# Four edits to the planner and the loads of a fused attention and MoE kernel: longer planned transfers, filling products on another bank, loads noted two pairs ahead, one-column operations that exclude nothing

## The chip, the cores and the metric

The kernel runs on one core of one Trainium2 chip. The metric is device time in microseconds (us), taken as the median of 3 runs of the kernel. A separate profiled execution gives the trace; its times below count from the first instruction of its span. Engines are named as the profile names them: PE (TensorE matmul), PEld (TensorE weight load), DVE (VectorE), ACT (ScalarE), POOL (GpSimd) and SP (SyncE, which issues every DMA here, one after the other).

## The reference

```
# q, k, v: (4 batches, 8 heads, 576 rows, 64); M_prev: (4, 8, 64, 64); z_prev: (4, 8, 64)
scores = q @ k.T / 8, causal mask, softmax (sum + 1e-9)      -> a
local = a @ v
phi(x) = max(x, 0) + min(exp(x), 1)
mem = (phi(q) @ M_prev) / (phi(q) @ z_prev + 1e-6)
x = gate * mem + (1 - gate) * local          # gate = sigmoid(beta) of each head
x as (2304 tokens, 512)
h = max(x @ w1, x @ w2, x @ w3)              # each w 512 x 768
out = h @ w_out                              # 768 x 512
```

All of it is in float32.

## The kernel before

**Work.** The 576 rows of a batch are cut into a first half of 320 rows and a second of 256. A "pair" is two heads of one half of one batch: 32 pairs, numbered 0 to 31 in the order batch, half, pair of heads, so that pairs 0 to 3 are the first half of batch 0, and pairs 8 to 11 the first half of batch 1. For each pair the kernel loads keys and queries (`load_qk`), transposes them, makes the scores of each head (tile `bs` in PSUM, the masked result and its least value by DVE, the exponential by ACT with its sum, a reciprocal by DVE, the scaling by POOL: tiles `p`, `st`, `sum`), transposes them (PE into `bt`, ACT copies to `pt`) and multiplies them with the values and the memory (`values`, PE into `bv`). What comes out is split into a high part `xh` and a low part `xl`. Pairs 0 to 3 use plain float32 products; from pair 4 on (SPLIT) operands are split into high and low parts; from pair 8 on (FLIP) keys and queries come through the ring `rw` of three buffers (12 transfers for a pair, 32 partitions each) and are turned by DVE (STREAM_TRANSPOSE into `rk`).

**The MoE of a half** can begin when all four of its pairs have their `xh` and `xl`. An "up" item is 12 products of one 128-column block into one PSUM bank, `bm`: three for each of the four pairs of heads (`xh,wh`, `xl,wh`, `xh,wl`). The items are spread between the steps of the next four pairs. Until all weights are there, all items use bank `bm[0]` alone.

**Weights** come in 24 chunks of 512 KB through the same ring `rw`. ACT scales a chunk into a `bm` bank, DVE rebuilds it there in three operations (the last writes `g`), ACT rounds it to `wh` and POOL takes the rest into `wl`. The first 8 chunks (SPREAD, L363) take the three `bm` banks in turn, the later ones only `bm[1]` and `bm[2]` (L550). Six chunks are noted in the steps of pairs 1 to 4, one more with each item of the MoE.

**Order.** Nothing is issued as the code runs: `Plan` notes each operation with what it depends on and a price (`cost`, `move`), and `emit` then plays all five engines forward in planned time and writes out each engine's instructions in that order. An operation is placed as soon as the plan has its inputs ready; the order of noting only decides between those that are ready. Each engine then runs its list in order, so a wrong price in the plan makes an engine wait at an instruction for which others stand ready behind it. L319 gives a transfer its planned landing, L201 its planned time in the DMA engines, `shares` (L204) says which DVE and POOL operations the plan doesn't let run together. Where the plan has PE idle for over 400 ns, L301 puts in small products of no use ("filling products", L300 in the profile) until the first real operation on the tensor that they write has come. Every other instruction of the plan has line L320 in the profile.

Of the kernel before, what the change touches and what calls it, by code (L numbers as in the profile page):

```python
# [17 lines left out]
PSUM = bass.MemoryType.PSUM  # L18


def f(ap):
    return ap.bitcast(F32)
# [45 lines left out]
class Plan:  # L68
# [119 lines left out]
    @staticmethod  # L188
    def move(*aps):

        piece, size = 512, 4
        for d in aps[0].shape:
            size *= d
        for ap in aps:
            run = 4
            for st, n in reversed(ap.ap if ap.space == bass.MemoryType.DRAM else ap.ap[1:]):
                if 4 * st != run:
                    break
                run *= n
            piece = min(piece, run)  # L200
        return size / 360 * (2 if piece < 512 else 1)  # L201

    @staticmethod
    def shares(eng, name, kw):  # L204

        if eng == "pool":
            return True
        if eng != "dve":
            return False
        aps = [a for a in kw.values() if isinstance(a, bass.AP) and a.shape[-1] > 1]  # L210
        inputs = [a for k, a in kw.items() if k in ("in_", "in0", "in1") and a.space != PSUM]
        if len(inputs) > 1:
            return True
        return name in ("tensor_scalar", "tensor_copy") and not any(a.space == PSUM for a in aps)

    def note(self, can):

# [40 lines left out]
    def emit(self):  # L258

        free = dict.fromkeys(self.ENGINES, 0.0)  # L260
        load = dict.fromkeys(self.ENGINES, 0.0)
        heaps = {e: [] for e in self.ENGINES}
        wait = {e: [] for e in self.ENGINES}
        dma = 0.0
        last = 0.0
        port = {"pool": 0.0, "dve": 0.0}
        other = {"pool": "dve", "dve": "pool"}

        def place(op):
            best = None  # L270
            for e, name, kw, cost in op.can:
                ready = max([0.0] + [
                    o.end + self.AFTER[o.eng][e] + self.SLACK * (e == "pe" and o.eng != "pe")
                    for o in op.deps
                ])
                done = max(ready, free[e] + load[e]) + cost + self.PEN.get(e, 0)
                if best is None or done < best[0]:
                    best = done, ready, (e, name, kw, cost)
            _, ready, (op.eng, op.fn, op.args, op.cost) = best
            load[op.eng] += op.cost  # L280
            heappush(wait[op.eng], (ready, op.prio, op.num, op))

        for op in self.ops:
            if not op.left:
                place(op)
        for _ in self.ops:
            start = {}
            for e in self.ENGINES:
                while wait[e] and wait[e][0][0] <= free[e]:
                    op = heappop(wait[e])[3]  # L290
                    heappush(heaps[e], (op.prio, op.num, op))
                if heaps[e]:
                    start[e] = free[e]
                elif wait[e]:
                    start[e] = wait[e][0][0]
            e = min(start, key=start.get)
            if e == "pe" and self.filler:
                free[e] = max(free[e], FILL_FROM)
                while start[e] - free[e] > FILL_GAP:
                    self.nc.tensor.matmul(**self.filler)  # L300
                    free[e] += 215 if free[e] < 4000 else 112  # L301
            if not heaps[e]:
                op = heappop(wait[e])[3]
            else:
                op = heappop(heaps[e])[2]
            op.at = start[e]
            if self.shares(e, op.fn, op.args):
                op.at = max(op.at, port[other[e]])
                port[e] = op.at + op.cost
            if e == "pe":  # L310

                w = op.args["in_" if op.fn == "transpose" else "lhsT"]
                last = op.at = max(op.at, last + 0.835 * w.shape[-1])
            load[e] -= op.cost
            if self.filler and op.args["out"].tensor.name == self.filler["out"].tensor.name:
                self.filler = None
            free[e] = op.end = op.at + op.cost
            if e == "sp":
                dma = op.end = max(op.end + 650, dma) + op.move  # L319
            getattr(getattr(self.nc, self.ENGINES[e]), op.fn)(**op.args)  # L320
            for u in op.users:
                u.left -= 1
                if not u.left:
                    place(u)
        return max(free.values())
# [20 lines left out]
def attention_memory_moe(ctx, tc, q, k, v, m_prev, z_prev, beta, w1, w2, w3, w_out, out):  # L346
# [11 lines left out]
    FLIP, XLOW, PHI, SPLIT = 8, 4, 4, 4  # L358


    EARLY_STEPS, PER_PIECE = range(3, 9), 1

    SPREAD = 8  # L363

    cp = ctx.enter_context(tc.tile_pool(name="cp", bufs=1))
    ps = ctx.enter_context(tc.tile_pool(name="ps", bufs=1, space=PSUM))
# [1 line left out]
    def tile_(shape, dtype, name):  # L368
        return cp.tile(shape, dtype, name=name)

    ident = tile_([128, 128], F32, "ident")
    mask = tile_([128, 448], F32, "mask")
# [39 lines left out]
    b_v = Ring(ps, 1, [128, 512], F32, "bv")  # L412
    bm = Ring(ps, 3, [128, 512], F32, "bm").tiles
# [11 lines left out]
    pairs = [(b, hi, hp) for b in range(B) for hi in range(2) for hp in range(NP)]  # L425
# [48 lines left out]
    def load_z(b):  # L474
        per_batch["z", b] = t = r_z.next()
        P.sp.dma_start(out=t, in_=z_prev[b : b + 1].broadcast_to([128, H, D]))

    def load_mv(b):

        per_batch["mv", b] = t = r_mv.next()  # L480
        P.sp.dma_start(out=t[:D], in_=m_prev[b].rearrange("h d e -> d h e"))
        P.sp.dma_start(out=t[D:], in_=v[b, :, 0:D, :].rearrange("h p d -> p h d"))

    def load_v(pi):
# [14 lines left out]
        out=mask[:, 320:],  # L499
# [43 lines left out]
    def load_weights(n):  # L543

        for _ in range(min(n, len(wchunks))):
            i = 4 * NF - len(wchunks)
            src, dh, dl = wchunks.popleft()
            t = r_w.next()
            g = r_g.next()
            bank = bm[i % 3 if i < SPREAD else 1 + i % 2]  # L550
            tv = t.rearrange("p (t x) -> p t x", t=NP) if len(src.shape) == 3 else t
            gv = g.rearrange("p (t x) -> p t x", t=NP) if len(src.shape) == 3 else g
            P.sp.dma_start(out=tv, in_=src)
            words = t.rearrange("p (x w) -> p x w", w=2)
            bits = bank.bitcast(U32)
            P.act.activation(out=bank, in_=f(words[:, :, 1]), func=AF.Copy, scale=2.0**-111)
            P.dve.tensor_scalar(
                out=bits, in0=bits, scalar1=3, scalar2=None, op0=ALU.logical_shift_left
            )
            P.dve.scalar_tensor_tensor(  # L560
                out=bits, in0=words[:, :, 0], scalar=29, in1=bits,
                op0=ALU.logical_shift_right, op1=ALU.bitwise_or,
            )
            P.dve.scalar_tensor_tensor(
                out=g.bitcast(U32), in0=words[:, :, 1], scalar=0x80000000, in1=bits,
                op0=ALU.bitwise_and, op1=ALU.bitwise_or,
            )
            P.act.copy(out=dh, in_=gv)
            P.pool.tensor_tensor(out=dl, in0=gv, in1=f(dh), op=ALU.subtract)
        if not wchunks and len(b_m.tiles) == 1:  # L570
            b_m.tiles += bm[1:]
            b_m.at = 1
# [348 lines left out]
    def run_moe(budget):  # L921
        while moe_q and budget > 0:
            c, fn = moe_q.popleft()
            load_weights(PER_PIECE)
            fn()
            budget -= c
        return budget
# [7 lines left out]
    transpose_in(0, "k")  # L935
    transpose_in(0, "q")
    debt = 0.0
    for n in range(nheads + 2):
        pieces = []
        sc = pt = None  # L940
        if n < nheads:
            pi, e = heads[n]
            us = HALVES[pairs[pi][1]].units
            sc = [(2 * u[3] * 0.425 + 100, partial(scores, pi, e, u)) for u in us]
            if HALVES[pairs[pi][1]].top and e == 0:
                sc.insert(0, (300, partial(scores_top, pi)))
            if e == 0:
                if pi + 1 < len(pairs):
                    load_qk(pi + 1)
                    b = pairs[pi + 1][0]  # L950
                    if b != pairs[pi][0]:
                        load_z(b)
                        load_mv(b)
        if n in EARLY_STEPS:
            load_weights(1)
# [9 lines left out]
        if n < nheads:  # L965
            pi, e = heads[n]
# [31 lines left out]
    run_moe(1e9)  # L998

    P.filler = dict(  # L1000
        out=b_v.tiles[0][:32, :64], lhsT=mask[:, :32], rhs=mask[:, :64], start=True, stop=True
    )
    P.emit()

# [29 lines left out]
```

## Time and profile before

| | before |
|---|---|
| median of 3 runs | 532.56 us (532.47 to 532.63) |
| the profiled execution | 532.99 us, its span 531.2 us |
| PE busy | 509.4 us, 96% of the span |
| DVE, ACT, POOL busy | 283.8, 336.1, 332.5 us |
| mean granted TensorE clock | 0.978 of 2.4 GHz |

The span is what the trace sees of the execution; 1.8 us lie around it. Busy PE is not PE at its peak: at the low clock the same product is busy for longer. The idle time of an engine costs nothing where another one is the bound.

### The profile page before, as it was taken

The page shows a single profiled execution, that of the slowest core. Times are in us where ns is not written, and L with a number is a line of the kernel's source. Part 1 is how long each engine was busy: PE and PEld are TensorE (multiplying, and loading weights), DVE is VectorE, ACT ScalarE, POOL GpSimd, SP SyncE. Part 2 cuts the span into 40 slices and gives each one's busy share as a digit, 9 for nine tenths or more (in the row PEclk, how much of TensorE's full clock was granted, in tenths as well). Part 3 has the DMA queues.
Part 4 walks back from the last instruction along what each step waited for, and adds up shares of the span by engine and source line. Part 5 has one row for each costly group of instructions (what it writes and reads, how often), then busy time and mean ns, then how long its engine had stood idle before and what let it go on. Part 6 is the DMA issues. An engine that isn't in the chain of part 4 may idle for free.

```text
span 531.2 us, 11153 instructions
## 1 busy us (share of the span) xinstructions
PE 509.4 (96%) x3602; PEld 445.1 (84%) x3602; DVE 283.8 (53%) x1048; ACT 336.1 (63%) x942; POOL 332.5 (63%) x505
## 2 busy tenths in 40 slices
PE   9879999989989899999999999999999999999997
PEld 7545687867978789998899889998899899997996
DVE  3667999987675354465455354445754454240110
ACT  4877989778676485577666586676776565533111
POOL 4777777888686475676787476677866554331110
PEclk9966999999999899999999999999999999999999
DMA  4846666664443564322442244231321110001001
GB/s 119 218 109 154 168 170 188 144 219 89 93 81 69 103 130 89 69 45 57 105 81 52 46 102 90 56 56 40 79 43 23 39 39 23 21 1 39 21 1 40
DMA packets 160090, 44.00 MB, mean 83 GB/s; under 512 B 147104, under 2 KB 156576, under 8 KB 160032
## 3 DMA queue, kind: packets, MB, share of 16 engines
q1 hardware_dynamic: 160032, 43.29, 35.7%
q8 instruction: 28, 0.46, 0.4%
q14 instruction: 30, 0.25, 0.2%
HBM read 38.54 MB, written 4.72 MB: 81 GB/s over the span
## 4 chain that ended last, share of the span: by engine, by line
PE 75%; ACT 6%; DMA 6%; DVE 4%; SPq 4%; issue 2%; POOL 2%; DVEq 0%; POOLq 0%; ACTq 0%
PE bm L320 49%; PE bv L320 9%; PE bt L320 8%; PE bs L320 8%; SPq L320 4%; DMA rw<-in_moe_w_dram 2%; DMA rw<-in_k_dram 1%; DMA rw<-in_q_dram 1%; ACT p L320 1%; PE bv L300 1%; ACT pt L320 1%; DVE g L320 1%; DVE bm L320 1%; ACT wh L320 1%; ACT k L320 1%
## 5 line engine op out<-in xcount | busy, mean ns | idle before, releaser
L320 PE MATMUL bm<-xh,wh 128*128 128x320 f32 (+1 forms) x576 | 178.3, 310 | 3.1 <-DVE t L320 2.2
L320 PE MATMUL bm<-xh,wl 128*128 128x320 f32 (+1 forms) x576 | 171.1, 297 | 0.0
L320 PE MATMUL bm<-xl,wh 128*128 128x320 f32 (+1 forms) x576 | 170.4, 296 | 0.0
L320 PEld LDWEIGHTS bm<-xh,wh 128*128 128x128 f32 x576 | 109.1, 189 | 9.4 <-DVE t L320 3.4
L320 POOL TENSOR_SCALAR p<-p,sum,gb 128x192 f32<-128x192 f32 (+3 forms) x128 | 87.5, 685 | 46.7 <-DVE sum L320 34.5
L320 PEld LDWEIGHTS bm<-xl,wh 128*128 128x128 f32 x576 | 109.2, 190 | 0.2
L320 PEld LDWEIGHTS bm<-xh,wl 128*128 128x128 f32 x576 | 109.0, 189 | 0.1
L320 ACT ACTIVATE p<-p,st 128x192 f32<-128x192 f32 (+4 forms) x144 | 84.7, 588 | 17.6 <-DVE st L320 16.6
L320 DVE TENSOR_TENSOR t<-bm,t 128x320 f32<-128x320 f32 (+1 forms) x96 | 43.4, 452 | 97.4 <-PE bm L320 97.0
L320 PE MATMUL bt<-ident,p 128*128 128x128 f32 x464 | 73.6, 279 | 11.5 <-ACT pt L320 7.9
L320 ACT COPY pt<-bt 128x384 f32<-128x384 f32 (+3 forms) x189 | 74.5, 417 | 10.9 <-PE bt L320 10.2
L320 DVE CUSTOM_DVE_ANT_0 p<-bs,mask 128x192 f32<-128x192 f32 (+3 forms) x128 | 60.1, 472 | 29.6 <-PE bs L320 28.8
L320 PEld LDWEIGHTS bt<-ident,p 128*128 128x128 f32 x464 | 56.4, 142 | 19.2 <-POOL p L320 6.9
L320 PE MATMUL bs<-k,qs 128*128 128x448 f32 (+2 forms) x336 | 69.9, 310 | 1.3 <-DVE st L320 1.1
L320 POOL TENSOR_TENSOR qs<-rk,qs 128x256 fp32r<-128x256 f32 (+1 forms) x42 | 34.2, 816 | 33.6 <-ACT qs L320 18.7
L320 PEld LDWEIGHTS bs<-k,qs 128*128 128x128 f32 x336 | 50.4, 186 | 4.7 <-DVE st L320 2.4
L320 POOL TENSOR_TENSOR hl<-t,hh 128x256 fp32r<-128x256 f32 x42 | 31.0, 739 | 34.1 <-ACT hh L320 34.1
L320 DVE STREAM_TRANSPOSE rk<-rw 128x320 f32<-128x320 f32 (+1 forms) x72 | 34.2, 476 | 30.0 <-POOL qs L320 10.6
L320 POOL TENSOR_TENSOR p<-phf,nn 128x128 f32<-128x128 f32 (+1 forms) x96 | 35.3, 373 | 18.0 <-PE bt L320 15.3
L320 ACT CAST qs<-rk 128x256 fp32r<-128x256 f32 (+1 forms) x47 | 20.1, 431 | 36.1 <-PE bs L320 35.3
L320 PE MATMUL bv<-pt,rv 128*64 128x256 f32 (+1 forms) x384 | 42.4, 352 | 0.0
L320 PEld LDWEIGHTS bv<-pt,rv 128*64 128x64 f32 x384 | 27.9, 141 | 16.9 <-issue 2.9
(91 smaller groups left out, 851.6 us busy)
## 6 DMA issues: line engine op xcount, KB each, us to landing
rw<-in_moe_w_dram SPq DMA_DIRECT2D x18, 512.0 KB, 4.6
rq<-in_q_dram SPq DMA_DIRECT2D x88, 64.0 KB, 2.5
rv<-in_v_dram SPq DMA_DIRECT2D x32, 128.0 KB, 2.9
rw<-in_q_dram SPq DMA_DIRECT2D x96, 40.0 KB, 2.1
out_dram<-g SPq DMA_DIRECT2D x15, 256.0 KB, 2.1
rw<-in_moe_w_out_dram SPq DMA_DIRECT2D x6, 512.0 KB, 4.2
rw<-in_q_dram SPq DMA_DIRECT2D x96, 32.0 KB, 2.0
rv<-in_v_dram SPq DMA_DIRECT2D x32, 64.0 KB, 2.3
```

Of the source, the lines that this page charges most:

```text
L300: self.nc.tensor.matmul(**self.filler)
L320: getattr(getattr(self.nc, self.ENGINES[e]), op.fn)(**op.args)
```

## The change

It makes five edits. `move` prices a transfer with long pieces at 240 bytes per ns where it had 360 (the price of short pieces, 180, stays). L319 lets a transfer land 1200 ns after its issue at the earliest, where it had 650. `shares` now says that an operation all of whose operands are one column wide excludes nothing. All weight chunks take banks `bm[1]` and `bm[2]`, so the first user of `bm[0]` is the MoE, and the filling products write `bm[0]`: they end at its first product instead of the first `values`. From pair 8 on, keys and queries are noted two pairs ahead.

```
-        return size / 360 * (2 if piece < 512 else 1)
+        return size / (180 if piece < 512 else 240)
@@ shares
-        return name in ("tensor_scalar", "tensor_copy") and not any(a.space == PSUM for a in aps)
+        return (
+            name in ("tensor_scalar", "tensor_copy")
+            and bool(aps) and not any(a.space == PSUM for a in aps)
+        )
@@ emit
-                dma = op.end = max(op.end + 650, dma) + op.move
+                dma = op.end = max(op.end + 1200, dma) + op.move
@@
-    SPREAD = 8
@@ load_weights
-            bank = bm[i % 3 if i < SPREAD else 1 + i % 2]
+            bank = bm[1 + i % 2]
@@
+    loaded = 1
@@
             if e == 0:
+                while loaded < min(len(pairs), pi + (3 if pi >= FLIP else 2)):
+                    load_qk(loaded)
+                    loaded += 1
                 if pi + 1 < len(pairs):
-                    load_qk(pi + 1)
                     b = pairs[pi + 1][0]
@@
     P.filler = dict(
-        out=b_v.tiles[0][:32, :64], lhsT=mask[:, :32], rhs=mask[:, :64], start=True, stop=True
+        out=bm[0][:32, :64], lhsT=mask[:, :32], rhs=mask[:, :64], start=True, stop=True
     )
```

All orders change. Three places follow, in each of which the numbers in a name tell the buffer.

**Place 1.** PE, after the `values` of pair 0, while pair 1's probabilities (`p`) are transposed and pair 2's scores (`kt,t`) begin. Before:

```order
L320 MATMUL bs_111<-kt_109,t_107 64x64 x2
L320 MATMUL bs_112<-kt_109,t_107 128x192
L320 MATMUL bt_114<-ident,p 128x128 x3
L320 MATMUL bt_113<-ident,p 128x128 x2
L320 MATMUL bs_111<-kt_109,t_107 128x320
L320 MATMUL bt_114<-ident,p 128x128 x3
```

The same place in the changed kernel:

```order
L323 MATMUL bs_111<-kt_109,t_107 64x64 x2
L323 MATMUL bs_112<-kt_109,t_107 128x192
L303 MATMUL bm_116<-mask 32x64 x5
L323 MATMUL bm_116<-xh_74,wh_66 128x320
L323 MATMUL bm_116<-xl_76,wh_66 128x320
L323 MATMUL bt_114<-ident,p 128x128 x3
L323 MATMUL bs_111<-kt_109,t_107 128x320
L323 MATMUL bs_112<-kt_109,t_107 128x192
L323 MATMUL bm_116<-xh_74,wl_69 128x320
L323 MATMUL bt_113<-ident,p 128x128 x2
```

Five filling products and the first three products of the first up item (of pair 0) now stand among the attention's. Three more stand behind each of the `values` of pairs 1 and 2, so 9 of the item's 12 products have moved ahead of the `values` of pair 3; before, none of them stood there. There are 61 filling products in all, where there were 60; 18 of them, not 15, stand ahead of the first transposes.

**Place 2.** ACT, around the sixth weight chunk (`bm_118<-rw_123`; the `wh` behind it is of the fourth), while pair 2's probabilities are copied to `pt`. Before:

```order
L320 ACTIVATE p,sum<-p,st 128x320
L320 ACTIVATE p,sum<-p,st 128x64
L320 COPY pt_126<-bt_113 128x3x128
L320 ACTIVATE bm_118<-rw_123 128x512
L320 CAST wh_66<-g_125 128x4x128
L320 ACTIVATE phe_90<-rq_94 128x4x64
L320 ACTIVATE p,sum<-p,st 128x192
L320 COPY pt_127<-bt_114 128x2x128
```

The changed kernel, from the copy to `pt_127` of the last row above on:

```order
L323 COPY pt_127<-bt_114 128x2x128
L323 ACTIVATE phe_90<-phe_90 128x4x64
L323 COPY pt_127<-bt_113 128x3x128
L323 CAST wh_66<-g_125 128x4x128
L323 CAST k_0_82<-bt_114 64x2x128
L323 CAST k_1_83<-bt_114 64x2x128
L323 ACTIVATE bm_118<-rw_123 128x512
```

The chunk's first operation has moved behind both copies to `pt_127`, the cast to `wh`, and two casts of keys. The first chunk's, likewise, moves behind four exponentials that stood after it.

**Place 3.** DVE, at the keys of pair 16 (`rk<-rw_123 128x320`), among the evictions of up items (`t_108<-bm`) and the masked scores (ISA `p,st<-bs`). Before:

```order
L320 STREAM_TRANSPOSE rk<-rw_123 128x256
L320 TENSOR_SCALAR sum<-sum 128x1
L320 RECIPROCAL sum<-sum 128x1
L320 TENSOR_TENSOR t_108<-bm_118,t_108 128x256
L320 STREAM_TRANSPOSE rk<-rw_123 128x320
L320 TENSOR_TENSOR t_108<-bm_116,t_108 128x256
L320 ISA p,st<-bs_112,mask 128x320
```

The changed kernel:

```order
L323 TENSOR_TENSOR t_108<-bm_118,t_108 128x256
L323 TENSOR_TENSOR t_108<-bm_116,t_108 128x256
L323 ISA p,st<-bs_112,mask 128x320
L323 ISA st 128x1
L323 STREAM_TRANSPOSE rk<-rw_121 128x256
L323 TENSOR_SCALAR sum<-sum 128x1
L323 RECIPROCAL sum<-sum 128x1
L323 STREAM_TRANSPOSE rk<-rw_123 128x320
L323 ISA p,st<-bs_111,mask 128x448
```

The keys of pair 16 are now turned behind one more eviction, one masked score and a sum that stood behind them. The keys of pairs 9 to 15 move in the same way, most of them by one or two evictions. On SP the pairs 9 to 17 keep the buffers of `rw` that they had, and come in the same turn.

## Rows read from the trace of the kernel before

**Rows 1.** The page's busy times, and PE, DVE and the clock in 40 slices of 13.3 us (tenths).

```profile
PE 509.4 (96%) x3602; PEld 445.1 (84%) x3602; DVE 283.8 (53%) x1048; ACT 336.1 (63%) x942; POOL 332.5 (63%) x505
...
PE   9879999989989899999999999999999999999997
...
DVE  3667999987675354465455354445754454240110
...
PEclk9966999999999899999999999999999999999999
```

**Rows 2.** Busy time by stretch: the stretch and its length in us, busy us (and instructions) of PE, PEld, DVE, ACT and POOL, granted clock, DMA share, GB/s.

```profile
24.00:27.40 3.40, 1.25 (x8) 0.69 (x8) 2.36 (x10) 3.38 (x12) 2.60 (x3) 0.99 1.15 293
27.40:37.60 10.20, 9.05 (x33) 5.15 (x33) 6.42 (x26) 7.59 (x19) 8.08 (x14) 0.50 0.42 108
...
41.00:51.20 10.20, 9.83 (x34) 4.96 (x32) 7.21 (x28) 6.69 (x20) 7.20 (x14) 0.50 0.57 155
57.00:130.00 73.00, 67.54 (x454) 57.44 (x450) 67.41 (x192) 61.20 (x152) 57.92 (x72) 1.00 0.62 164
142.00:191.00 49.00, 44.15 (x313) 38.60 (x313) 27.19 (x110) 29.50 (x95) 35.14 (x55) 0.97 0.47 87
181.00:184.40 3.40, 3.40 (x10) 2.62 (x9) 0.40 (x4) 0.76 (x2) 1.33 (x2) 0.51 0.55 109
191.00:488.00 297.00, 297.00 (x2152) 269.30 (x2150) 143.09 (x572) 189.59 (x534) 188.17 (x290) 1.00 0.27 56
```

**Rows 3.** The chain of work that ended last, in order of time: start us, us, what. `DMA rw` is a transfer on the chain; `bv` are `values`.

```profile
35.46 2.46 PE bv L320 x12
...
38.88 4.29 DMA rw<-in_moe_w_dram
...
47.04 2.60 PE bv L320 x12
...
175.82 2.41 DMA rw<-in_k_dram
...
190.84 1.34 PE bv L320 x12
...
267.48 1.44 PE bm L320 x12
...
470.41 1.76 PE bm L320 x12
```

**Rows 4.** ACT in order of time: start us, us, instruction, and in brackets its idle time before it and what ended that. The first is of the beta gates, the others of weight chunks one and six, and of `xh` of pair 1.

```profile
7.43 0.21 ACT L320 ACTIVATE gb<-gb 128x8 f32<-128x8 f32 x1 [1.46 <-DMA gb<-in_beta_dram]
...
20.51 0.63 ACT L320 ACTIVATE bm<-rw 128x512 f32<-128x512 f32 x1 [1.87 <-DMA rw<-in_moe_w_dram]
...
37.94 0.43 ACT L320 CAST xh<-bv 128x320 fp32r<-128x320 f32 x1 [1.03 <-PE bv L320]
...
43.20 0.63 ACT L320 ACTIVATE bm<-rw 128x512 f32<-128x512 f32 x1 [2.04 <-DMA rw<-in_moe_w_dram]
```

**Rows 5.** PE in order of time, columns as in rows 4: the opening filling products, then the waits around 27 and 40 us, the first `values` of pair 3, and two waits of stretch 142 to 191 us.

```profile
0.98 3.41 PE L300 MATMUL bv<-mask 128*32 128x64 f32 x30 [0.98 <-DVE mask L495]
...
27.45 0.88 PE L320 MATMUL bt<-ident,p 128*128 128x128 f32 x3 [1.76 <-ACT pt L320]
...
39.97 0.52 PE L320 MATMUL bt<-ident,p 128*128 128x128 f32 x3 [1.36 <-ACT pt L320]
...
56.67 0.76 PE L320 MATMUL bv<-pt,mv 128*64 128x320 f32 x4
...
165.13 0.52 PE L320 MATMUL bt<-ident,p 128*128 128x128 f32 x3 [1.28 <-ACT pt L320]
...
179.87 0.52 PE L320 MATMUL bt<-ident,p 128*128 128x128 f32 x3 [1.85 <-ACT pt L320]
```

**Rows 6.** DVE in order of time, columns as in rows 4: the low part `xl` of pair 1, a one-column sum, then keys and queries turned.

```profile
38.40 0.49 DVE L320 TENSOR_TENSOR xl<-bv,xh 128x320 fp32r<-128x320 f32 x1 [0.59 <-ACT xh L320]
...
39.37 0.15 DVE L320 TENSOR_SCALAR sum<-sum 128x1 f32<-128x1 f32 x1
...
142.01 0.51 DVE L320 STREAM_TRANSPOSE rk<-rw 128x320 f32<-128x320 f32 x1 [2.69 <-DMA rw<-in_q_dram]
...
161.91 0.45 DVE L320 STREAM_TRANSPOSE rk<-rw 128x256 f32<-128x256 f32 x1 [2.81 <-DMA rw<-in_k_dram]
...
170.18 0.45 DVE L320 STREAM_TRANSPOSE rk<-rw 128x256 f32<-128x256 f32 x1 [1.61 <-DMA rw<-in_k_dram]
...
178.36 0.51 DVE L320 STREAM_TRANSPOSE rk<-rw 128x320 f32<-128x320 f32 x1 [3.19 <-DMA rw<-in_k_dram]
```

**Rows 7.** POOL in order of time, columns as in rows 4, at the sum of rows 6.

```profile
39.03 1.27 POOL L320 TENSOR_TENSOR wl<-g,wh 128x512 fp32r<-128x512 f32 x1 [1.63 <-ACT wh L320]
```

**Rows 8.** SP in order of time, columns as in rows 4: transfers issued for pair 9 (the first two rows) and pair 16 (the third).

```profile
119.04 1.84 SPq L320 DMA_DIRECT2D rw<-in_k_dram  x4
120.92 5.20 SPq L320 DMA_DIRECT2D rw<-in_q_dram  x8
...
173.35 2.93 SPq L320 DMA_DIRECT2D rw<-in_k_dram  x4
```

**Rows 9.** DMA issues: names, issuer, count, KB each, median us from issue to landing.

```profile
rw<-in_moe_w_dram SPq DMA_DIRECT2D x18, 512.0 KB, 4.6
...
rw<-in_q_dram SPq DMA_DIRECT2D x96, 40.0 KB, 2.1
```

## The prediction

> **What bounds the kernel now.** The page's slices come first [rows 1]. PE is busy 96% of the span and from the fifth slice on almost without a hole; its clock is low in the third and fourth slice only, and DVE is at nine tenths for four slices (53 to 106 us) and low later. So three stretches have to be told apart, and the table by stretch does it [rows 2].
>
> From 191 to 488 us PE is busy 297.0 of 297.0 us at full clock. Nothing that another engine does there is worth anything, and the change neither adds nor takes away a product of the MoE. What it can win or lose lies ahead of 191 us:
>
> - *Stretch 1, to 57 us.* No MoE product runs, since the four pairs of batch 0's first half aren't through. From 27.4 to 37.6 and from 41.0 to 51.2 us the granted clock is 0.50 (1.2 GHz), each time after PE had stood in holes: it was busy 1.25 of the 3.40 us ahead of the first fall. The holes end with ACT's copy to `pt` (1.76 us at 27.45, 1.36 us at 39.97 [rows 5]). ACT itself waits for weight chunks that haven't landed, 1.87 us at 20.51 and 2.04 us at 43.20 [rows 4]; the second of these transfers is on the chain, 4.29 us from 38.88 [rows 3].
> - *Stretch 2, 57 to 130 us.* PE is busy 67.5 of 73 us and DVE 67.4: weights are rebuilt on DVE beside the scores, and the two share the bound.
> - *Stretch 3, 142 to 191 us.* PE is busy 44.15 of 49 us, so 4.85 us idle, while no engine else is full (POOL, the next, 35 us). The holes follow one pattern: DVE stands at a transpose of keys or queries whose transfer hasn't landed (2.69, 2.81, 1.61 and 3.19 us [rows 6]), ACT stands behind it in its own order, and PE behind ACT's `pt` (1.28 us at 165.13, 1.85 us at 179.87 [rows 5]). The transfer before the last of them is on the chain, 2.41 us from 175.82 [rows 3]. After the last hole the clock is at 0.51 for 3.4 us [rows 2], which costs 3.4 x 0.49 = 1.7 us. So 6.5 us lie here.
>
> **The change part by part.**
>
> *Planned landing.* With 475 ns for the issue and 1070 ns to the waiting engine, the plan had 512 KB land and be used after 475 + 650 + 1456 + 1070 = 3.65 us, and now after 475 + 1200 + 2184 + 1070 = 4.93 us; the trace has 4.6 [rows 9]. For a 40 KB piece of queries it goes from 2.42 to 2.97 us, where the trace has 2.1 as a median; but the four late ones of [rows 6] show that the tail is what hurts. So the plan was too early for weights and is now slightly late for both, and later in an in-order list means that other work stands ahead of the wait. This is the edit that I expect the gain from.
>
> *Stretch 1, ACT's two waits: -2.0 us.* In the changed order the first chunk stands behind four more exponentials and the sixth behind two copies, three casts and more (place 2). Both waits, 3.91 us, then lie beside work. ACT is not alone on the chain, though: PE, POOL and DVE take turns there, and 7.59 of 10.2 us are the work of ACT itself [rows 2]. Bounds are 0 and 3.9; I take half.
>
> *Nine products pulled ahead: -1.3 us.* They ran after 57 us, at 1.76 us for 12 [rows 3], so 9 are 1.3 us less in stretch 2. Where they stand now they fill PE's holes if their inputs are there in time; the price if they aren't is a rival. Bounds 0 and 1.3 for the gain.
>
> *Filling products: 0.* There are 61 for 60. Three more stand ahead of the first transposes, 2 x 3.41/30 = 0.23 us each [rows 5], so 0.7 us; but ACT, behind the copy that these transposes feed, stands 1.46 us until the transfer of beta has come [rows 4], and that covers them. Without this cover: +0.7. Five more stand in the hole ahead of 27.45 us and hold only 1.1 us of it.
>
> *Clock in stretch 1: 0.* The same `values` take 2.46 and 2.60 us at half clock and 1.34 at full [rows 3]. If the clock stayed up, those two alone give 2.4 us, and no more than 20.4 - 7.59 - 6.69 = 6.1 us can come, as ACT's own work remains [rows 2]. Whether some five filling products and two real ones keep it up no row shows. The holes of 1.8 and 1.4 us shrink but don't go, so I take 0 and make the rest a rival.
>
> *Bank of the weights: 0.* Two banks for three in the first 8 chunks. The later 16 chunks run on two already, in the stretch where DVE is the bound, so a third bank isn't what they lack; in stretch 1 chunks wait for transfers, not banks. Bounds: 0 and one scaling by ACT, 0.63 us [rows 4].
>
> *One-column operations: 0.* The sum at 39.37 us ran its 0.15 us [rows 6] inside a POOL subtraction that lasted from 39.03 to 40.30 [rows 7], so excluding the two was a price that the chip doesn't take; the edit moves sums ahead in the plan by a POOL instruction at most. [...]
>
> *Two pairs ahead: 0.* A transfer goes out when its buffer is free, whatever its turn in the notes, and `rw` has three buffers as before. SP issues for pair 9 at 119.04 and pair 16 at 173.35 [rows 8], seven pairs in 54.3 us or 7.8 us a pair, and its list keeps that turn. The edit only decides between transfers that are ready together. Bounds: one group of four issues either way, 1.9 us [rows 8], in a stretch that has PE work to cover it.
>
> *Stretch 3, transposes later: -3.6 us.* Each moves behind at least one more eviction of an up item (place 3), and 12 products of 256 columns take 1.44 us [rows 3]. Of the four waits (10.3 us) 1.4 us each go, 5.7 us or 55%; 55% of 6.5 us are 3.6. Bounds 0 and 6.5. What is late next is ACT's cast of the keys, which comes 1.4 us later too, but the keys are for scores a pair or more ahead.
>
> *Stretch 2: 0.* DVE's work is the same but for some ten copies and subtractions that pass between ACT, POOL and DVE. Bounds are the idle 5.5 us of PE as a gain, and 3 us (as many as DVE's busiest five such, 0.5 us each) as a loss.
>
> *Sum.* -2.0 - 1.3 - 3.6 = -6.9 us. The profiled execution's own time is 532.99 us (span 531.2 and 1.8 around it), so 526.1; it lies 0.43 above the median, so **525.7 us** for the median.
>
> **The rivals.**
>
> *The clock stays up in stretch 1 (chance 0.20).* For it: the fall came behind holes in which now something stands. Against it: holes remain. It gives 4 us more, between 2.4 and 6.1: 521.7 us.
>
> *Only stretch 1 gains (0.20).* SP issues without a break from 119 us on; if the transposes' transfers slip as far as the transposes, the waits form again. Then 3.6 us are missing: 529.3 us.
>
> *Nothing moves (0.08).* DVE, full for 92% of stretch 2, swallows what stretch 1 brings, and stretch 3 stays: some 0.5 us, 532.1.
>
> *Slower: the nine products hold PE (0.15).* PE runs its list in order, and the products stand ahead of the next pair's transposes. Each triple needs `xh` and `xl` of the pair before. Pair 1's `values` end at 37.92 [rows 3], its `xl` at 38.89 [rows 6], and ACT now does chunks and exponentials ahead of `xh`: say 1.6 us for each of three triples, and nine products at half clock, 0.29 us each, 2.6 us. That is 7.4 us in front of attention, whose `p`, `pt` and scores all wait for PE, and ACT's saved waits vanish behind it. Against 1.3 + 3.6 won elsewhere it leaves +2.5: 535.1 us. It decides from a hold of 4.9 us on. Against it: PE stood 1.36 us at just this place anyway [rows 5], waiting for `pt`.
>
> **How the numbers follow.** The forecast has the remaining 0.37, with its own range of 522 to 530 (half of the three terms missing, or the upper bounds of two). The difference that a measurement here can tell from none is about 0.2%, 1.07 us: faster is below 531.5. Faster has 0.37 + 0.20 + 0.20 = 0.77, same 0.08, slower 0.15. The range of 519 to 533 holds the first four cases and leaves out the slower one and a clock that gives its 6 us beside a full stretch 3.
>
> **What would show it.** ACT's waits at the first and sixth chunk are gone. The `values` of pair 3, which end stretch 1, begin some 2 us earlier than 56.67 [rows 5], with 9 products on `bm` ahead of them. The waits of DVE at `rk` between 140 and 180 us shrink to under half, PE's idle time in that stretch to some 2 us, and the low clock near 181 us is gone. From there PE is full, and the end moves by the sum. I am wrong if PE waits for `xl` or `wl` at the early products, if the two low stretches of the clock change in length, or if the transposes stand as long as before at later places.

## The result and the profile after

The changed kernel takes **523.29 us** (median of 4 runs, 522.55 to 524.74), the one before 532.51 us beside it (4 runs): a ratio of 0.9833, 95% interval 0.9808 to 0.9859. The profiled execution took 523.83 us, its span is 522.0 us. The forecast was 525.7 us. The sum is near; the experiments show that its terms are not.

The busy times and the slices of the changed kernel's page, which answer to [rows 1]:

```profile
PE 504.4 (97%) x3604; PEld 443.3 (85%) x3604; DVE 296.5 (57%) x1064; ACT 331.7 (64%) x931; POOL 328.5 (63%) x500
...
PE   9988899989998999999999999999999999999997
...
DVE  4999999998555465455654475446654444330120
...
PEclk9998899999998999999999999999999999999999
```

DVE is now at nine tenths from the second slice on, where it had been at 6 and 7; it is busy for 12.7 us more in all, ACT for 4.4 less. The same by stretch (columns as in [rows 2]), first the piece that had been at half clock, then the two short pieces that are now:

```profile
27.40:37.60 10.20, 8.18 (x48) 4.83 (x48) 9.72 (x35) 9.55 (x28) 9.34 (x14) 1.00 0.77 215
43.60:47.00 3.40, 3.28 (x14) 2.52 (x12) 3.40 (x13) 2.67 (x10) 2.81 (x5) 0.50 0.87 223
53.80:57.20 3.40, 3.18 (x13) 3.02 (x14) 2.95 (x12) 2.06 (x6) 1.88 (x4) 0.50 0.80 197
57.00:130.00 73.00, 69.58 (x471) 59.31 (x470) 68.31 (x194) 59.90 (x152) 60.48 (x78) 1.00 0.57 150
135.00:182.00 47.00, 44.11 (x313) 38.98 (x313) 24.00 (x100) 28.51 (x91) 32.74 (x51) 0.96 0.46 85
159.60:163.00 3.40, 3.40 (x18) 3.36 (x17) 1.45 (x7) 2.32 (x8) 3.11 (x6) 0.51 0.47 86
182.00:478.00 296.00, 296.00 (x2144) 268.62 (x2142) 149.72 (x579) 186.32 (x531) 183.88 (x286) 1.00 0.28 58
```

From 182 us on PE is full, as before from 191 us on. So all of the gain lies ahead, and one can read it from when the `values` of a pair begin, if as many products of the MoE stand ahead of them. That is so at pair 4 (36 products), pair 8 (300) and pair 11 (504). PE of the changed kernel, first `values` of pairs 3, 4, 8 and 11:

```profile
49.65 0.76 PE L323 MATMUL bv<-pt,mv 128*64 128x320 f32 x4
...
64.65 0.65 PE L323 MATMUL bv<-pt,mv 128*64 128x256 f32 x4
...
135.13 0.49 PE L323 MATMUL bv<-pt,mv 128*64 128x320 f32 x2
...
181.46 0.76 PE L323 MATMUL bv<-pt,mv 128*64 128x320 f32 x4
```

The kernel before has pairs 4 and 8 at

```profile
69.44 0.65 PE L320 MATMUL bv<-pt,mv 128*64 128x256 f32 x4
...
142.36 0.49 PE L320 MATMUL bv<-pt,mv 128*64 128x320 f32 x2
```

and pair 11 at 190.8 (its piece of the chain in [rows 3] begins at 190.84). The gain is 4.8 us by pair 4, 7.2 by pair 8 and 9.3 by pair 11. Pair 3 comes 7.0 us earlier than at 56.67 [rows 5], but with 9 products ahead of it; from there to pair 4 the changed kernel takes 15.0 us for 27 products, where the one before took 12.8 us for 36. At the places that the prediction spoke of:

- *ACT* waits 0.86 us for the first chunk where it waited 1.87 [rows 4], and at no other chunk ahead of pair 3; beta's wait of 1.46 us is 0.23.

```profile
6.76 0.21 ACT L323 ACTIVATE gb<-gb 128x8 f32<-128x8 f32 x1 [0.23 <-DMA gb<-in_beta_dram]
...
19.84 0.63 ACT L323 ACTIVATE bm<-rw 128x512 f32<-128x512 f32 x1 [0.86 <-DMA rw<-in_moe_w_dram]
```

- *PE* stands at the first product of three triples until `xh` has come, 3.2 us in all. Two of them are early ones, of pairs 1 and 2 (2.45 us); pair 0's doesn't wait, and the third wait belongs to pair 3's triple, which stands behind the `values` of pair 3. These waits are new, and are of the kind that the slower rival named:

```profile
33.62 0.41 PE L323 MATMUL bm<-xh,wh 128*128 128x320 f32 x1 [1.81 <-ACT xh L323]
...
41.95 0.41 PE L323 MATMUL bm<-xh,wh 128*128 128x320 f32 x1 [0.64 <-ACT xh L323]
...
52.98 0.42 PE L323 MATMUL bm<-xh,wh 128*128 128x320 f32 x1 [0.73 <-ACT xh L323]
```

- *DVE* still waits for keys and queries in stretch 3, 7.4 us at these four (and 0.4 at a fifth) where [rows 6] had 10.3:

```profile
136.92 0.51 DVE L323 STREAM_TRANSPOSE rk<-rw 128x320 f32<-128x320 f32 x1 [0.94 <-DMA rw<-in_q_dram]
...
139.87 0.45 DVE L323 STREAM_TRANSPOSE rk<-rw 128x256 f32<-128x256 f32 x1 [2.20 <-DMA rw<-in_k_dram]
...
156.16 0.45 DVE L323 STREAM_TRANSPOSE rk<-rw 128x256 f32<-128x256 f32 x1 [2.95 <-DMA rw<-in_k_dram]
...
173.90 0.51 DVE L323 STREAM_TRANSPOSE rk<-rw 128x320 f32<-128x320 f32 x1 [1.32 <-DMA rw<-in_k_dram]
```

- *The clock* is low for 10.2 us in all (the last microsecond left out), where it was for 23.9 [rows 2]; the low piece near 181 us is gone, but one of the same length stands at 159.6 us, behind the longest of these waits.

### The profile page after: what moved, and what is told of

Read it like the earlier page. It is cut to its first block, busy times and chain, and to the rows that moved or that the text cites. A ratio compares the mean times of both kernels' runs of the same rounds, so it can differ in the third digit from the quotient of the medians.

```text
span 522.0 us, 11139 instructions
## 1 busy us (share of the span) xinstructions
PE 504.4 (97%) x3604; PEld 443.3 (85%) x3604; DVE 296.5 (57%) x1064; ACT 331.7 (64%) x931; POOL 328.5 (63%) x500
## 4 chain that ended last, share of the span: by engine, by line
PE 78%; ACT 6%; DVE 6%; DMA 3%; SPq 3%; issue 2%; POOL 1%; DVEq 0%; ACTq 0%; POOLq 0%
PE bm L323 52%; PE bt L323 9%; PE bv L323 8%; PE bs L323 8%; SPq L323 3%; PE bm L303 2%; DVE bm L323 1%; ACT p L323 1%; ACT pt L323 1%; DVE g L323 1%; DMA rw<-in_moe_w_dram 1%; ACT k L323 1%; DMA rw<-in_k_dram 1%; DMA rw<-in_moe_w_out_dram 1%; DVE p L323 1%
## 5 line engine op out<-in xcount | busy, mean ns | idle before, releaser
L323 DVE TENSOR_TENSOR t<-bm,t 128x320 f32<-128x320 f32 (+1 forms) x96 | 43.6, 454 | 102.7 <-PE bm L323 102.4
L323 ACT COPY pt<-bt 128x384 f32<-128x384 f32 (+3 forms) x182 | 72.1, 416 | 13.5 <-PE bt L323 13.0
L323 PE MATMUL bs<-k,qs 128*128 128x448 f32 (+2 forms) x336 | 72.2, 315 | 1.6 <-DVE st L323 1.3
L323 POOL TENSOR_TENSOR qs<-rk,qs 128x256 fp32r<-128x256 f32 (+1 forms) x41 | 32.9, 802 | 32.6 <-ACT qs L323 16.4
L323 POOL TENSOR_TENSOR hl<-t,hh 128x256 fp32r<-128x256 f32 x44 | 32.4, 737 | 32.4 <-ACT hh L323 32.4
L323 POOL TENSOR_TENSOR p<-phf,nn 128x128 f32<-128x128 f32 (+1 forms) x96 | 36.6, 386 | 20.1 <-PE bt L323 17.5
L323 ACT CAST hh<-t 128x256 fp32r<-128x256 f32 x48 | 19.5, 406 | 36.3 <-DVE t L323 36.0
L323 PE MATMUL bv<-pt,rv 128*64 128x256 f32 (+1 forms) x384 | 41.0, 345 | 0.0
```

## The experiments

Ratios are to the kernel before on the same chip (530.6 us in the first four runs, 530.75 and 530.9 us in the others), each with its 95% interval. "Clock low" is how long the granted clock was 0.5 in the profiled execution. The columns of pairs 4, 8 and 11 say when, in that execution, their first `values` began (us); a "lap" is the time between the first `values` of two pairs. These times can differ by some 2 to 4 us between two profiles of nearly the same program (e3 moves no median, yet has pair 11 at 187.1 us), so a verdict rests on the ratio, and the laps say where.

| | ratio | pair 4 | pair 8 | pair 11 | clock low, us |
|---|---|---|---|---|---|
| before | 1 | 69.4 | 142.4 | 190.8 | 23.9 |
| changed | 0.9833 | 64.6 | 135.1 | 181.5 | 10.2 |
| e1 prices alone | 0.9960 [0.9931, 0.9989] | 68.6 (24 products) | 139.9 | 187.1 | 23.9 |
| e2 bank and filling alone | 0.9961 [0.9935, 0.9986] | 68.3 | 139.6 | 185.2 | 17.1 |
| e3 two pairs ahead alone | 0.9992 [0.9969, 1.0015] | 67.6 | 140.9 | 187.1 | 17.1 |
| e4 one-column rule alone | 0.9889 [0.9855, 0.9923] | 64.6 | 139.4 | 181.7 | 13.7 |
| e5 the rule, order only | 0.9854 [0.9823, 0.9885] | 68.0 | 137.9 | 180.8 | 23.9 |
| e6 the rule, engines only | 1.0066 [1.0043, 1.0089] | 72.5 (24) | 146.3 | 193.7 | 34.1 |
| e7 changed, without the rule | 0.9922 [0.9895, 0.9949] | 68.0 | 137.9 | 185.2 | 17.1 |
| e8 changed, no early products | 0.9740 [0.9719, 0.9762] | 61.7 | 130.2 | 175.3 | 0 |
| e9 e8, filling ends early | 0.9776 [0.9762, 0.9790] | 61.3 | 130.9 | 177.0 | 10.2 |
| e10 e8, prices back | 0.9807 [0.9771, 0.9843] | 64.3 | 135.2 | 179.8 | 3.4 |
| e11 e8, rule back | 0.9832 [0.9817, 0.9847] | 65.5 (24) | 136.7 | 179.5 | 3.4 |

**e1: the two transfer prices alone.**

```
-        return size / 360 * (2 if piece < 512 else 1)
+        return size / (180 if piece < 512 else 240)
-                dma = op.end = max(op.end + 650, dma) + op.move
+                dma = op.end = max(op.end + 1200, dma) + op.move
```

> The kernel before with the two transfer prices alone. The prediction put 2.0 us of ACT's chunk waits and 3.6 us of the late transposes here: it expects 526.9 us, with DVE's waits for keys and queries between 140 and 180 us at half. The rival, that these waits form again wherever the transposes stand and the gain came from elsewhere, expects 530.5 to 532.5 us.

0.9960, some 2 us: the rival's range. The prediction had given this edit most of its sum, 5.6 us. DVE's waits for keys and queries from 140 to 180 us came to 7.2 us, not to half of 10.3.

**e2: bank of the weights and of the filling products alone.**

```
-            bank = bm[i % 3 if i < SPREAD else 1 + i % 2]
+            bank = bm[1 + i % 2]
-        out=b_v.tiles[0][:32, :64], ...
+        out=bm[0][:32, :64], ...
```

> The kernel before with the weight bank and the filling products' tensor changed, nothing else. The prediction expects the nine early products alone: 531.2 us. The rival that the clock holds through stretch 1 expects 527 to 529 us, with one low stretch of the clock gone; the rival that the early products hold PE expects over 533.5 us.

0.9961. The predicted 531.2 us are a ratio of 0.9975, which the interval holds; both rivals lie outside it. Here too 9 products run ahead of pair 3's `values` (at 55.3 us), and PE waits for `xh` at one of them alone, 0.5 us.

**e3: two pairs ahead alone.**

```
-                    load_qk(pi + 1)
+                while loaded < min(len(pairs), pi + (3 if pi >= FLIP else 2)):
+                    load_qk(loaded)
+                    loaded += 1
```

> The kernel before with keys and queries noted two pairs ahead from pair 8 on, nothing else. The prediction expects no difference (532.5, within 1 us), as the buffers of the ring decide when a transfer goes out. The rival, that the turn of the notes decides in the stretch where SP issues without a break, expects 529 to 531 us and shorter waits of DVE for transfers between 140 and 180 us.

0.9992, an interval that holds 1: nothing, as predicted.

**e4: the one-column rule alone.**

```
-        return name in ("tensor_scalar", "tensor_copy") and not any(a.space == PSUM for a in aps)
+        return (
+            name in ("tensor_scalar", "tensor_copy")
+            and bool(aps) and not any(a.space == PSUM for a in aps)
+        )
```

> The kernel before with the one-column rule alone. The prediction put it at nothing: 532.5 us, within 1 us. The rival: all 288 sums and reciprocals are freed from standing behind POOL in the plan, which shortens the chain exponential, sum, scaling, transposes of every step in stretch 1, where latency is the bound; it expects 526 to 530 us, with the values of pair 3 beginning 3 us or more before 56.7 us.

0.9889, the largest part by far, the rival's range, and the prediction had put it at 0; pair 3 comes at 52.6 us. What the rule frees are the 144 sums alone: `shares` never held the reciprocals. The four ratios multiply to 0.980, so the parts together (0.983) give no more than their product.

**e5 and e6: the rule's two effects apart.** With the rule on, 45 of the 648 operations that two engines may take change engine, and all orders change. A list of letters holds each of the 648 on one engine (the same for both, with the list of before in e5 and that of e4 in e6; e6 keeps the old `shares`):

```
+        op.pick = next(self.picks) if len(can) > 1 else op.eng[0]
...
             for e, name, kw, cost in op.can:
+                if len(op.can) > 1 and e[0] != op.pick:
+                    continue
```

> The kernel before with the one-column rule, but every operation that two engines may take (648 of them: copies and subtractions) is held on the engine that it had in the kernel before. So only the order within the engines changes. The one-column rule alone gave 0.989. If its gain is the order (the plan no longer holds POOL or DVE back behind operations that on the chip exclude nothing), this run keeps it: 0.987 to 0.992, with values of pair 3 near 53 us and of pair 11 near 182 us. If its gain is that some copies pass from ACT to DVE, this run loses it: 0.997 to 1.003, values of pair 3 near 56 us. If it is a matter of chance which order comes out of a small edit, it lies anywhere, with no relation to the other run of this pair.

> The counterpart: the kernel before with its old rule of exclusion, but each of the 648 operations that two engines may take is held on the engine that it gets under the one-column rule (45 of them differ). If the gain is the order, this run stays at 0.997 to 1.003. If it is the shift of copies from ACT to DVE, this one has it: 0.987 to 0.992, with ACT busy 3 to 5 us less. If each gives about half, both lie near 0.994.

The order alone is 0.9854, the engines alone 1.0066: the gain is the order, and the 45 operations that change engine (9 of them from ACT to DVE) are no part of it; alone they make the kernel slower than either branch had it. Expected was pair 3 of e5 near 53 us; it came at 56.6, though with 8 products ahead of it, so e5 gains by another path than e4. Its `values` of pairs 8 and 11, and PE's busy time in three stretches, the first at half clock (columns as in [rows 2]):

```profile
137.94 0.49 PE L339 MATMUL bv<-pt,mv 128*64 128x320 f32 x2
...
180.80 0.49 PE L339 MATMUL bv<-pt,mv 128*64 128x320 f32 x2
```

```profile
27.30:51.20 23.90, 22.62 (x78) 12.55 (x77) 17.75 (x66) 18.43 (x55) 17.48 (x29) 0.50 0.55 153
56.60:137.90 81.30, 78.92 (x544) 67.20 (x543) 72.20 (x220) 68.42 (x180) 67.58 (x89) 1.00 0.62 159
137.90:180.80 42.90, 41.33 (x308) 36.94 (x308) 24.69 (x97) 27.86 (x90) 31.61 (x50) 1.00 0.48 87
```

The kernel before in the last two of these:

```profile
56.70:142.40 85.70, 80.24 (x554) 68.77 (x553) 72.71 (x214) 69.84 (x179) 65.28 (x84) 1.00 0.61 156
142.40:190.80 48.40, 43.55 (x310) 38.17 (x309) 26.60 (x110) 29.37 (x94) 34.94 (x55) 0.96 0.47 87
```

PE was idle 5.46 + 4.85 us there and is idle 2.38 + 1.57 us in e5. What PE waited for (us in all, times, longest) from 57 to 142 us, first of before, then of e5:

```profile
PE bm L320 <- DVE t L320: 3.0, 4, 1.0
```

```profile
PE bm L339 <- DVE t L339: 0.2, 1, 0.2
```

So in e5 the evictions of the MoE's products come in time. That is the path of this order and not of the rule everywhere: e4, with the rule and its own choice of engines, still waits for them.

```profile
PE bm L323 <- DVE t L323: 2.5, 3, 1.2
```

Of e4's gain 4.9 us lie ahead of pair 4 and 6.1 between pairs 8 and 11, and it loses 1.9 between pairs 4 and 8.

How often the plan of before held a sum can be counted: DVE's sums share a turn with POOL 144 times, and at 98 of these the plan lets DVE stand until POOL's operation is through, 34.6 us of planned time in all, 7.8 of it in the plan's first 60 us. The chip doesn't stand there: the sums take 144 ns in the mean over the run, and by the records 143 ns both for the 73 that lie wholly inside one POOL operation and for the 37 that meet none.

```profile
L320 DVE TENSOR_SCALAR sum<-sum 128x1 f32<-128x1 f32 x144 | 20.6, 144 | 38.1 <-ACT p L320 37.2
```

That the order gains is shown. That it gains because these holds are gone is argued, from their count and from a gain of 0.9 to 1.5% in all four pairs of kernels that differ by the rule (e4 and e5 here, e7 and e11 below). The third branch, chance, is not ruled out by a control: no run changed the order in a way that should mean nothing, and e6 shows that such a shift can be worth 0.7%.

**e7: the changed kernel with e4's edit taken back.**

> The changed kernel with the one-column rule taken back. If the rule's gain is its own (alone 0.989 of before, the other three parts together 0.991 by the product of their runs alone), this run lies at 0.989 to 0.993 of before, 1.006 to 1.010 of the changed kernel, and values of pair 11 come 3 to 4 us later than in the changed kernel. If the parts win the same holes, so that one does what the other would have done, it stays at 0.983 to 0.986.

0.9922, the first branch: the rule is worth 0.9% beside the other parts. The laps put 3.3 us of it ahead of pair 4; at pair 11 it is 3.8.

**e8: the changed kernel without early products.**

```
-        for kt in range(NP):
+        for kt in reversed(range(NP)):
             for a, x in ((wh, xh), (wh, xl), (wl, xh)):
```

> The changed kernel with the pairs of heads of every up item taken in the opposite turn, 3 to 0 for 0 to 3. Then no product of the MoE can stand ahead of the values of pair 3, and filling products, which need no input, fill those holes until then (126 for 61). The arithmetic is the same but for the order of sums. If the nine early products are what holds the clock up and gives the gain of stretch 1, the low stretches grow from 6.8 us to some 20 us ahead of pair 3 and the time is 526 to 528 (0.989 to 0.992 of before). If any PE work holds the clock and the early products only cost waits for their inputs (3.2 us in the changed kernel), values of pair 3 come at 47 to 48.5 us for 49.7, nine products are then still to run (1.3 us), and the time is 521 to 523.5 (0.979 to 0.984). If neither counts, as holes there are ended by ACT and DVE, it is the nine products alone: 1.3 us more, 0.985 to 0.987.

0.9740, faster than expected by any branch, and 0.9% faster than the changed kernel. It has 108 filling products, not the 126 expected. The clock stays at full speed to the end, and pair 4 comes 2.9 us earlier with as many products ahead. Two things had changed at once; the next run parts them.

**e9: e8 with filling products that end at the first `values`.**

```
-        out=bm[0][:32, :64], ...
+        out=b_v.tiles[0][:32, :64], ...
```

> The kernel of e8 (up items in the opposite turn, 0.974 of before) with the filling products back on the bank of the values, so that they end at the first values near 21 us and the holes from there to pair 3 stay empty; nothing else differs. It separates the two things that e8 did at once. If the filling products behind 21 us hold the clock and that is the gain of e8, the low stretches come back (17 to 24 us ahead of pair 3, none in e8), values of pair 3 come near 53 to 55 us, and the time is 522 to 526 (0.984 to 0.991). If what e8 gained is that PE no longer stood before the early products (3.2 us in the changed kernel), the clock may fall, but the time stays at 517 to 519 (0.974 to 0.978).

0.9776, in the time of the second branch: most of e8's gain over the changed kernel comes of the turn of the up items and not of the filling products. That it comes by PE's waits for `xh` isn't shown. The laps of the changed kernel from pair 1 to 2 and from pair 3 to 4, then those of e9 (columns as in [rows 2]):

```profile
29.60:38.79 9.19, 6.90 (x41) 3.98 (x40) 8.71 (x34) 8.74 (x25) 8.27 (x12) 1.00 0.68 187
...
49.65:64.65 15.00, 12.88 (x78) 10.60 (x77) 13.76 (x46) 13.53 (x36) 10.92 (x15) 0.89 0.60 166
```

```profile
29.27:38.61 9.34, 7.83 (x40) 4.14 (x40) 8.93 (x37) 8.97 (x27) 8.49 (x13) 0.87 0.78 216
...
47.79:61.31 13.52, 12.59 (x88) 10.83 (x87) 13.43 (x49) 13.42 (x36) 11.00 (x16) 1.00 0.62 163
```

The longest of the waits, 1.81 us, lies in the first of these laps, which is no longer than in e9 (nor than e8's 9.73). From 28.8 to 43.3 us the chain of the changed kernel runs through ACT, DVE and a transfer, and through PE neither at this wait nor at the one at 41.95 us. Around the longest it is:

```profile
33.54 0.21 SPq L323
...
33.80 2.62 DMA rq<-in_q_dram
...
36.43 0.56 DVE nn L323
```

The changed kernel falls behind from pair 2 to 3 (10.86 us for e9's 9.18) and from pair 3 to 4, where it does 9 products fewer in 1.5 us more. What of this is order, and what the low clock at 43.6 and 53.8 us, stays open. Pairs 3 and 4 of e8, then of e9:

```profile
48.20 0.49 PE L323 MATMUL bv<-pt,mv 128*64 128x320 f32 x2
...
61.73 0.65 PE L323 MATMUL bv<-pt,mv 128*64 128x256 f32 x4
```

```profile
47.79 0.49 PE L323 MATMUL bv<-pt,mv 128*64 128x320 f32 x2
...
61.31 0.65 PE L323 MATMUL bv<-pt,mv 128*64 128x256 f32 x4
```

And the low clock of e9:

```profile
28.00:31.40 3.40, 3.40 (x15) 1.62 (x15) 3.40 (x9) 3.32 (x10) 3.22 (x6) 0.50 0.93 303
38.30:41.70 3.40, 3.40 (x16) 1.67 (x16) 3.19 (x11) 2.73 (x9) 3.22 (x7) 0.50 0.76 218
154.30:157.70 3.40, 3.40 (x18) 3.40 (x18) 1.62 (x10) 2.36 (x10) 2.99 (x6) 0.50 0.45 84
```

With 6.8 us of low clock ahead of pair 3, e9 is there no later than e8 with none. The two programs differ in filling products alone, the last four of them behind pair 3's `values`; e9 falls behind only between pairs 4 and 11, by 1.05 us to pair 8 and by 1.08 more to pair 11, where the low piece at 154.3 us lies. Whether that piece comes of the missing filling products or of how transfers landed in this execution isn't settled.

**e10: e8 with e1's edit taken back.**

> The kernel of e8 with the two transfer prices as before (650 ns, and 360 bytes per ns for long pieces). Alone the prices gave 0.996. If that gain stands beside the others, this run is at 0.977 to 0.979 of before. If the filling products and the one-column rule have already won the holes that late transfers left, it is at 0.973 to 0.976. If the later transposes of keys cost more than they save under the new order (stretch 3 took 42.3 us with the one-column rule alone, 46.4 in the changed kernel), it is faster than e8: under 0.973, with values of pair 11 within 44 us of those of pair 8.

0.9807, slower than any branch had it, though the interval reaches into the first: the prices are worth 0.7% here, by the intervals not clearly more than alone (0.4%). The laps show 2.6 us ahead of pair 4 and 2.4 more to pair 8, but from pair 8 to 11 this kernel takes 44.6 us and e8 takes 45.1, while DVE's waits for keys and queries there are 7.3 us here and 5.4 in e8. So in these profiles none of the prices' gain lies in stretch 3, where the prediction had put most of it, and shorter waits of DVE don't come with a shorter stretch.

**e11: e8 with e4's edit taken back.**

> The kernel of e8 without the one-column rule. The rule was worth 1.1 per cent alone and 0.9 on top of the other parts. If its gain is the order of DVE and POOL in all three stretches, it costs the same here though the clock is held by filling products: 0.982 to 0.986 of before. If a part of it was the clock (24 us low before, 13.7 with the rule alone), and filling products give that anyway, 0.977 to 0.980. If it is gone here, 0.973 to 0.976.

0.9832, the first branch: the rule is worth 0.9% also where the clock is hardly low (3.4 us here).

## Why the prediction was right in sum and wrong in its terms

*What held.* All of the gain lies ahead of the stretch where PE is full, and that stretch is worth nothing. Two pairs ahead: 0 (e3). ACT's wait at the sixth chunk is gone and that at the first is halved. The opening filling products are covered, as beta's wait shrank by 1.23 us. The time lies 2.4 us under the forecast. All three signs that the prediction named for being wrong came true, though: PE waited at early products (for `xh`), the two low stretches of the clock changed in length, and the transposes stood as long at other places. Pair 3 came 7.0 us earlier, not some 2.

*One-column operations: 0. This is the step that failed.* That the chip doesn't hold a sum back was read rightly from [rows 6, 7]. The conclusion was wrong: "the edit moves sums ahead in the plan by a POOL instruction at most". At most a POOL instruction each, but 98 times; and what follows on DVE, and what waits for it on PE and ACT, is planned late too and can be placed behind other work. With all edits DVE stands much less: from the `values` of pair 0 to those of pair 4 it is busy for 40.5 of 43.2 us, before for 37.8 of 47.3. The edit is worth 1.1% alone (e4), 0.9% beside the others (e7, e11), some 5 to 6 us, and it is an effect of order (e5) and not of engines (e6). By which of its changes of order it gains stays open: e4 and e5 gain in different laps.

*Nine early products: -1.3 us. In the changed kernel their turn costs time.* The term took the products out of stretch 2 and costed their place ahead of pair 3 at nothing; the price, had `xh` been late, was left to the slower rival. `xh` was late at two of the three early triples, 2.45 us, and at pair 3's. e9, which differs from the changed kernel by the turn of all up items, five filling products and the order that follows from the turn, is 0.6% faster, about 3 us, and has pair 4 earlier by 3.3 us. The rival's hold of 7.4 us was too long, and the longest wait lies off the chain, so the cost came otherwise than the rival had it. On the kernel before, the same nine products stand in a gain (e2).

*Stretch 3: -3.6 us. The place and the size were wrong.* The transposes still wait 7.4 us at four places, not under half of 10.3. From pair 8 to 11 the changed kernel takes 46.3 us for 48.4, of which the prices account for little: 1.2 us alone (e1, 47.2 us), none in e10. The step let each transpose slip by one eviction, 1.4 us, and took the transfers as fixed; the traces show waits of the same size at other places (2.95 us at 156.16). That was named as a rival, "only stretch 1 gains".

*ACT's two chunk waits: -2.0 us.* The waits went by 1.01 and 2.04 us. In the sum, the prices gained 2.6 us ahead of pair 4 on top of e8 (e10), near the term; alone they showed nothing certain there (e1 had 12 products fewer ahead of pair 4).

*The clock.* The rival said that a clock that stays up gives 4 us more, 521.7 us. It did stay up for most of stretch 1 (low for 6.8 us where it was for 20.4), and the time, 523.3, lies between it and the forecast; but the runs speak against the rival's price. e5 is at half clock for 23.9 us, as long as before, and gains 1.5%; e9 is low for 10.2 us, as long as the changed kernel, and is 0.6% faster. In e9 the low pieces hold the `values` of pairs 1 and 2, from which the rival took 2.4 us (the first four products of each take 1.33 us and more, 0.76 in e8), and e9 reaches pair 3 no later than e8 without any low clock: there the slow products fill holes that PE has in any case. So the term of 0 holds up to pair 3 for these two kernels. Behind it, e8 with its filling products is 0.4% faster than e9, and in e5 PE was busy for 22.6 of the 23.9 us at half clock; what the clock costs there no run shows.

*The bank: 0.* e2 is 0.4% faster, 2 us, with bank, filling products and nine early products in one; what of this each gives was not measured.

Of the 6.9 us forecast the prices gave some 2 alone (e1) and 3.5 on top of e8's parts (e10), about half of that in stretch 2, where none was looked for; the turn that puts the products early took some 3 away; and the edit that counted for nothing brought 5. That the sum came near was luck: errors of both signs met.

## What to carry to other kernels

In a kernel whose order a planner makes, count how often the plan holds an operation for a wrong price before calling the price small: here 98 holds of at most one instruction each stood behind a term that was put at 0, and the edit that removed them was worth some 5 us. Work pulled ahead into the holes of an engine that runs its list in order can cost more than the holes were worth; the turn of one loop decided it here, and the opposite turn makes the best kernel of the study (e8, 0.974 of before). A wait, or a low clock, counts where it lies on the chain: the longest new wait of the changed kernel did not, nor did e9's low clock ahead of pair 3.

## What the runs showed of the hardware

The exclusion that the rule dropped for one column does hold for other small DVE operations. The product of `nn` with the gates has two inputs in SBUF and 4 or 6 columns, the one that makes the gates (`gb`) has one input and 8 columns. DVE and, below it, POOL of the kernel before, in order of time:

```profile
7.67 0.17 DVE L320 TENSOR_SCALAR gb<-gb 128x8 f32<-128x8 f32 x1 [1.53 <-ACT gb L320]
...
8.12 0.84 DVE L320 TENSOR_SCALAR gb<-gb 128x8 f32<-128x8 f32 x1
...
43.17 0.16 DVE L320 TENSOR_TENSOR nn<-nn,gb 128x6 f32<-128x6 f32 x1
...
60.73 1.20 DVE L320 TENSOR_TENSOR nn<-nn,gb 128x4 f32<-128x4 f32 x1
```

```profile
8.07 0.85 POOL L320 TENSOR_TENSOR k<-kt,k 64x320 fp32r<-64x320 f32 x1 [5.36 <-ACT k L320]
...
60.62 1.28 POOL L320 TENSOR_TENSOR wl<-g,wh 128x512 fp32r<-128x512 f32 x1
```

At 43.17 us POOL does nothing and 6 columns take 0.16 us. At 60.73 us POOL's subtraction has just begun, and 4 columns take 1.20 us: they end at 61.93, right behind POOL's 61.90. A sum of one column with one input, inside just such a subtraction, took 0.15 us [rows 6, 7]. The Trainium skill (SBUF — State Buffer, "SBUF: two separate sides") says that a DVE operation with two SBUF inputs and a GpSimd operation that reads SBUF hold a shared pair of ports one at a time, for a whole instruction; for two inputs the trace agrees (1.20 us for 0.16). With one input, 8 columns take 0.17 us at 7.67 us, where POOL does nothing, and 0.84 us at 8.12, where they begin inside POOL's subtraction and end at 8.96, right behind its 8.92. The sums are the same operation (TENSOR_SCALAR) with one input too, and aren't held: so it is their width of one column, not the number of inputs, that sets them apart. From which width on one input is held, between 2 and 8 columns, no run shows.
